# A fused attention and feed-forward kernel: plain float32 for fewer products, and a new order of work

## The chip, the cores and the metric

One core of a Trainium2 chip runs the whole program. It has five engines with a queue each: TensorE (PE, matmuls and transpositions into PSUM banks; its weight loads are listed as PEld), VectorE (DVE), ScalarE (ACT), GpSimd (POOL) and SyncE (SP, which here only issues transfers). An engine works through its queue in order, and an instruction that waits holds up everything behind it. The metric is the device time of one execution in microseconds (us), less being better.

## The reference

Block-causal attention over q, k, v of shape (8, 8, 576, 64), and on its output a feed-forward part with a convolution of three rows and a gate:

```python
scores = (1.0 / np.sqrt(D)) * np.matmul(q, k.transpose(0, 1, 3, 2))
mask = block_i >= block_j                       # blocks of 64 rows
scores = np.where(mask, scores, -1000000000.0)
attn = np.exp(scores - np.max(scores, axis=-1, keepdims=True))
attn = attn / (np.sum(attn, axis=-1, keepdims=True) + 1e-09)
x = np.matmul(attn, v)                          # heads side by side: (8, 576, 512)
h = np.maximum(x @ w_in, 0.0)                   # w_in (512, 1024)
conv_out = sum(conv_w[k] * hp[:, k:k + S, :] for k in range(3))
out = (h * (1.0 / (1.0 + np.exp(-conv_out)))) @ w_out   # w_out (1024, 512)
```

The three weight arrays come as 64-bit floating point numbers, q, k and v as float32.

## The kernel before

**Numbers in two halves.** TensorE reads a float32 operand either as plain float32 or under a rounded type, float32r. Where the kernel uses the rounded type it keeps an operand as a high half (rounded) and a low half (what rounding left), and adds three products: high by high, high by low, low by high. The tiles have names that end so: `wih`, `wil` are the halves of w_in, `woh`, `wol` of w_out, `ptah`, `ptal`, `ptbh`, `ptbl` of the transposed attention weights, `vv` holds the high half of v in columns 0 to 63 and the low half in 64 to 127.

**Visits.** The work goes pair by pair of heads, four pairs for each of the eight batch elements. The first batch element is done in two rounds, so that its feed-forward part can start early: in the first visits (part "A") each of the four pairs does its query rows 0 to 255, in the second visits (part "B") rows 256 to 575; the 28 pairs of the other batch elements have one visit each. A visit transposes q and k (`first_t`, `rest_t`, `stage_t`), forms the scores and exponentials (`stage_sa`, `stage_sb`, `stage_s`), normalizes them on POOL, transposes the weights back (`stage_x`, L1564) and multiplies them by v (`stage_pv`). Two first visits and two second visits work on both heads at once. In the first and second visits every product of q and k, and P V (L1648), is plain float32: `early` is true there. The later visits use halves (L1672, L1668).

**Feed-forward.** `ffn` runs for rows 0 to 254 of batch element 0 after its first visits, for its other rows after the second visits, then twice for each batch element. L1754 multiplies x by the halves of w_in (12 matmuls for each of eight chunks of 128 columns), ACT and DVE do the gate, POOL the low half `gl` (L1794), and L1820 multiplies by the halves of w_out.

**Weights.** `split` turns each 64-bit weight tile into halves. SP loads it (L1105, L1131), ACT takes absolute values (L976), POOL clamps (L982, for all but the first tile), DVE shifts bits (L987, L999, L1003, L1010), ACT writes the high half (L1045); then TensorE forms minus the high half (L1061) and the remainder (L1064) in a bank. For four of the sixteen tiles (`WPA`) it also adds the number itself by a plain float32 matmul (`all_`, L1070) and ACT writes the low half (L1073); for the others DVE adds the number while it writes the low half (L1067).

**The first loads.** The first 256 rows of q and k for all eight heads go into one tile under the name `ptbh`, and v into `ptbl` (`load_first`, L943, L954); TensorE transposes q and k as plain float32 against `ident` (L1260).

**What sets the order.** Every operation is entered in a plan (`pl.op`) with its engine, a duration, what it depends on, and the buffers it touches. `Plan.order` then places all of them: it keeps one list of ready operations for each engine and takes the one with the smallest due time from a table of numbers (`TARGETS`, one for each operation, in twentieths of a us). A PE operation whose mark `rows64` differs from that of the one before is lengthened by `switch` (0.2). Where the plan leaves PE idle for longer than `LEAST` (0.4 us), and a bank is free, it puts filling matmuls there, whose results nobody reads (`work`, L1969). So the order of each engine's queue is fixed before the program runs; what an instruction waits for on the chip is another matter.

Of the kernel before, what the change touches and what calls it, by code (L numbers as in the profile page):

```python
# [580 lines left out]
def kernel(  # L581
# [70 lines left out]
    QDV, KDV, RDV, ADV, BDV, LDV = (), (), (), (), (), False  # L652
    EA = True
    WPE = tuple(range(16))
    WPA = (0, 1, 2, 3)
    VAT = (0, 1, None, 0)
    FHP = ()
    ZDMA, APM, SHARE = True, True, {0: 2}
# [72 lines left out]
    def twin(tag):  # L731
# [4 lines left out]
        if len(hist) > cap:  # L736
            b.before = hist[-1 - cap]
# [1268 lines left out]
```

## Time and profile before

| | us |
|---|---|
| median of three runs | 757.05 |
| lowest and highest of them | 756.24, 759.91 |
| the profiled execution | 758.76 |
| its span, first to last instruction | 756.9 |
| TensorE busy | 748.3 |
| VectorE busy | 622.2 |
| ScalarE busy | 604.0 |
| GpSimd busy | 418.9 |
| ten filling matmuls of the start (L1969, `blank`) | 4.6 |
| twenty later ones (L1969, `rident`) | 6.6 |

The span begins with the first instruction, and the profiled execution's own time has 1.9 us around it. A row of the timeline gives the start in us, the length in us, the engine, the line, the operation, what it writes and reads, its shape, how many like it follow directly (x10), and in brackets the idle time before it with what ended that. Lengths of matmuls overlap, since they are pipelined; what one costs is read from the distance between starts. A plain float32 matmul shows as two records, one of the rounded type as one. A row of a group gives the count, then busy us and the mean ns of one, then idle us before.

### The profile page before, as it was taken

Reading aid. Unit: us, or ns where it says so; the run is one execution under the profiler, and the core shown is the slowest. Engines: PE = TensorE matmul, PEld = TensorE weight load, DVE = VectorE, ACT = ScalarE, POOL = GpSimd, SP = SyncE. Lnnn points to the kernel's source line nnn. Section 1 sums busy time; section 2 is a strip of 40 time slices with the busy share of each in tenths; the row PEclk is TensorE's granted clock in tenths of the full one; section 3 lists DMA queues with packets and bytes.
Section 4 is the critical chain, followed back from the end, with each engine's and each line's share of the span. In section 5 each row is a group of like instructions: output and inputs, shape, how many; then the busy total and the mean of one; then the engine's idle time right before and its main releaser. Section 6 shows DMA issues by size and latency. Waiting matters only on the chain.

```text
span 756.9 us, 16715 instructions
## 1 busy us (share of the span) xinstructions
PE 748.3 (99%) x5155; PEld 669.0 (88%) x5155; DVE 622.2 (82%) x1831; ACT 604.0 (80%) x1753; POOL 418.9 (55%) x630
## 2 busy tenths in 40 slices
PE   8899999999999999999999999999999999999998
PEld 5577789899999898999989899998989889898997
DVE  5879889998979788898979879898889879896541
ACT  6879979878979688797979679797978769786652
POOL 2435365666765546566565547556575655665321
PEclk9999999999999999999999999999999999999999
DMA  8754665577562555465454664555456544530001
GB/s 223 207 155 143 164 125 122 129 163 166 127 148 69 132 136 130 106 157 129 116 118 107 143 146 110 122 131 125 112 131 144 126 115 115 127 75 15 15 29 42
DMA packets 165628, 92.63 MB, mean 122 GB/s; under 512 B 134924, under 2 KB 142116, under 8 KB 165540
## 3 DMA queue, kind: packets, MB, share of 16 engines
q1 hardware_dynamic: 164996, 91.43, 49.6%
q8 instruction: 42, 0.69, 0.4%
q14 instruction: 46, 0.38, 0.2%
q10 hardware_dynamic: 544, 0.13, 0.1%
HBM read 38.30 MB, written 9.44 MB: 63 GB/s over the span
## 4 chain that ended last, share of the span: by engine, by line
PE 94%; ACT 2%; DVE 2%; POOL 1%; issue 0%; ACTq 0%; POOLq 0%
PE bank L1820 27%; PE bank L1754 26%; PE bank L1672 11%; PE bank L1564 8%; PE bank L1377 5%; PE bank L1375 4%; PE bank L1648 3%; PE bank L1329 3%; PE bank L1179 3%; PE bank L1969 1%; PE bank L1420 1%; PE bank L1061 1%; PE bank L1064 1%; DVE st L1496 0%; PE bank L1325 0%
## 5 line engine op out<-in xcount | busy, mean ns | idle before, releaser
L1754 PE MATMUL bank<-x,wih 128*128 128x290 f32 (+3 forms) x1024 | 200.9, 300 | 0.0
L1794 POOL TENSOR_TENSOR gl<-t,gh 128x289 fp32r<-128x289 f32 (+3 forms) x128 | 103.2, 811 | 127.6 <-ACT gh L1791 118.1
L1754 PEld LDWEIGHTS bank<-x,wih 128*128 128x128 f32 x1024 | 158.0, 189 | 3.5 <-issue 0.8
L1820 PE MATMUL bank<-woh,gh 128*128 128x512 f32 (+1 forms) x296 | 118.3, 400 | 0.0
L1820 PE MATMUL bank<-woh,gl 128*128 128x512 f32 (+1 forms) x296 | 115.0, 388 | 0.0
L1820 PE MATMUL bank<-wol,gh 128*128 128x512 f32 (+1 forms) x296 | 114.9, 388 | 0.0
L1754 PE MATMUL bank<-x,wil 128*128 128x290 f32 (+3 forms) x512 | 111.3, 299 | 0.0
L1385 DVE TENSOR_REDUCE st<-bank 128x1 f32<-128x128 f32 (+1 forms) x224 | 106.3, 482 | 2.9
L1578 DVE TENSOR_TENSOR ptbl<-bank,ptbh 128x512 fp32r<-128x512 f32 (+1 forms) x140 | 87.6, 631 | 5.5 <-ACT ptbh L1575 3.1
L1575 ACT ACTIVATE ptbh<-bank 128x512 fp32r<-128x512 f32 (+2 forms) x168 | 81.4, 503 | 9.5 <-PE bank L1564 8.7
L1775 DVE SCALAR_TENSOR_TENSOR t<-bank,cw,t 128x289 f32<-128x289 f32 (+3 forms) x128 | 64.8, 506 | 23.8 <-ACT t L1771 22.1
L1754 PEld LDWEIGHTS bank<-x,wil 128*128 128x128 f32 x512 | 82.3, 189 | 0.8 <-issue 0.4
L827 POOL TENSOR_SCALAR vv<-vn 128x320 fp32r<-128x320 f32 x56 | 25.7, 460 | 90.2 <-DMA vn<-in_v_dram 51.9
L1377 PE MATMUL bank<-kl,qz 128*128 128x128 f32 (+1 forms) x224 | 71.8, 322 | 0.0
L1820 PEld LDWEIGHTS bank<-woh,gl 128*128 128x128 f32 x296 | 55.5, 188 | 12.4
L1771 ACT ACTIVATE t<-bank,cw 128x289 f32<-128x289 f32 (+3 forms) x128 | 64.2, 501 | 2.7
L1779 DVE SCALAR_TENSOR_TENSOR t<-bank,cw,t 128x288 f32<-128x288 f32 (+3 forms) x128 | 64.1, 501 | 1.1
L1768 ACT ACTIVATE bank<-bank 128x290 f32<-128x290 f32 (+3 forms) x128 | 51.7, 404 | 15.6 <-PE bank L1754 14.6
L1791 ACT ACTIVATE gh<-t 128x289 fp32r<-128x289 f32 (+3 forms) x128 | 56.0, 444 | 8.9 <-DVE t L1787 7.9
L1784 ACT ACTIVATE t<-t 128x289 f32<-128x289 f32 (+3 forms) x128 | 56.9, 445 | 7.3 <-DVE t L1779 6.5
L1672 PE MATMUL bank<-ptbl,vv 128*64 128x192 f32 x224 | 61.5, 315 | 0.0
L1820 PEld LDWEIGHTS bank<-wol,gh 128*128 128x128 f32 x296 | 55.8, 189 | 5.6
(187 smaller groups left out, 2005.0 us busy)
## 6 DMA issues: line engine op xcount, KB each, us to landing
out_dram<-stage SPq DMA_DIRECT2D x35, 256.0 KB, 2.2
ka<-kh SPq DMA_DIRECT2D x56, 144.0 KB, 2.6
kb<-kh SPq DMA_DIRECT2D x56, 144.0 KB, 2.6
vn<-in_v_dram SPq DMA_DIRECT2D x58, 128.0 KB, 2.7
qnf<-in_q_dram SPq DMA_DIRECT2D x56, 128.0 KB, 2.4
knf<-in_k_dram SPq DMA_DIRECT2D x56, 128.0 KB, 2.7
x<-in_moe_w_out_dram SPq DMA_DIRECT2D x8, 512.0 KB, 4.4
qa<-qh SPq DMA_DIRECT2D x28, 144.0 KB, 2.4
```

Source lines behind the costliest of these rows:

```text
L1377: nc.tensor.matmul(sb.ap[:, 0:nk], qz.ap[:, z:z + 128], kl.ap[:, 0:nk], start=False, stop=True)
L1385: nc.vector.tensor_reduce(out=st.ap[:, i:i + 1], in_=sb.ap[:, 0:nk], op=ALU.max, axis=AX.X, negate=True)
L1564: nc.tensor.matmul(tb.ap[0:kk, col:col + P].bitcast(F32R), pb[x].raw[:, 128 * c:128 * c + kk], rident, start=(z == 0), stop=True, is_trans ...
L1575: nc.scalar.activation(out=hi(), in_=src(), func=AF.Copy)
L1578: nc.vector.tensor_tensor(out=lo(), in0=src(), in1=hi(), op=ALU.subtract)
L1672: nc.tensor.matmul(tb.ap[0:m, q0 - qa:qb - qa], vv.ap[:, chunk(c), w[ps_]], pm.ap[:, 128 * c + q0:128 * c + qb] if qa == 0 else pm.ap[:, c ...
L1754: nc.tensor.matmul(fb.ap[:, 0:n2], wt[:, c, fs], xs[c][xi].ap[:, x0:x0 + n2], start=(n + c - c0 == 0), stop=(n + c - c0 == 3 * NCC - 1))
L1771: nc.scalar.activation(out=t.ap[:, 0:no], in_=fb.ap[:, own:own + no], func=AF.Copy, scale=cw[:, NFC + f:NFC + f + 1])
L1775: nc.vector.scalar_tensor_tensor(out=t.ap[:, i0:no], in0=fb.ap[:, own + i0 - 1:own + no - 1], scalar=cw[:, f:f + 1], in1=t.ap[:, i0:no], o ...
L1779: nc.vector.scalar_tensor_tensor(out=t.ap[:, 0:i1], in0=fb.ap[:, own + 1:own + 1 + i1], scalar=cw[:, 2 * NFC + f:2 * NFC + f + 1], in1=t.a ...
L1794: nc.gpsimd.tensor_tensor(out=gbuf[1].ap[:, f, carry:carry + no], in0=t.ap[:, 0:no], in1=gbuf[0].ap[:, f, carry:carry + no], op=ALU.subtract)
L1820: nc.tensor.matmul(fb.ap[:, 0:cut], gbuf[a].ap[:, f, cs], w[:, f, ds], start=(f == 0 and n == 0), stop=(f == NFC - 1 and n == 2))
```

## The change

The table `TARGETS` is new throughout, so that the order differs on every engine from the start to shortly before the end. Beside it:

- `PRB`: in the second visits only pairs 0 and 1 keep the plain float32 P V. Pairs 2 and 3 get halves of the weights and of v: v is loaded into `vn`, POOL writes its halves into `vv` in three cuts of rows, ACT writes the high half of the transposed weights, and the low half comes either from DVE or (for the two blocks of 384 and 512 columns, `EBLK`) from a matmul that subtracts the high half in the bank (`sub`) and an ACT copy. P V is then three passes.
- `WPA` is empty: no plain float32 matmul for weight tiles (`all_`) is left, and DVE writes all low halves (`fl2`).
- The first q and k lie where the exponentials of the second visits go later (from `p2` on), under two names, float32 and float32r; they are transposed under the second. The first exponentials of `p2`, `p3`, `p4` wait for those transpositions.
- `rows64` gets a value for each kind of plain float32 matmul (2 or 3), so that the plan counts `switch` at every change of type; before it did so only around the scores of the first two rounds. The plan's time for a transfer of a w_in tile goes from some 1.6 to 1.9 us.
- New branches with `SRAW` or `PRA` false aren't taken.

Instructions over the whole program, before and after: plain float32 matmuls of P V 56 and 36, of weight sums 5 and 0; rounded matmuls for P V of the second visits 0 and 56, subtractions (`sub`) 0 and 8; filling matmuls 30 and 36; transpositions of the first q and k 16 and 16 (plain, then rounded); low-half copies of attention weights on ACT 0 and 8, of w_in tiles on ACT 5 and 0, their additions on DVE 4 and 9; passes over v on POOL 112 and 124; transfers on SP 769 and 769.

```diff
-139 133 161 153 228 245 108 134 154 173 261 282 282 276 548 557 342 446 499 534 561 522 556 540 613 602 185 233 212 248 362 494 247 263 252 264 271 254 321
...
-    WPA = (0, 1, 2, 3)
+    WPA = ()
     VAT = (0, 1, None, 0)
+    SRAW, PRA, PRB = True, True, (0, 1)
...
+    qkt = [nc.alloc_sbuf_tensor_at(f"qk{x}", [P, 2, 2, H, D], d, offset=at0).ap() for x, d in (("f", F32), ("r", F32R))]
+    firstq = Bin([])
...
+        elif tag in ("p2", "p3", "p4"):
+            b.before = firstq
...
-        vn = vraw(VAT[p]) if part else one([P, 5, 2, D], F32, "vn")
+        vn = vraw(VAT[p]) if part and p in PRB else one([P, 5, 2, D], F32, "vn")
...
+        if part and p not in PRB:
+            return halves((0, 1), VCUT)
...
-        bufs, vbufs = [[late(j, hh) for hh in range(2)] for j in range(2)]
+        bufs, vbufs = [firstq], [late(1, hh) for hh in range(2)]
...
-        ld = pl.op(SP, 0.4 if f < NFC else 1.0, go, (at - WLEAD if f >= NFC else WL0 + WLS * f) + JD[f], deps=deps, bufs=bufs, xfer=c_dma(P * 4096 // share, 1024) if f < NFC else 2.1)
+        ld = pl.op(SP, 0.4 if f < NFC else 1.0, go, (at - WLEAD if f >= NFC else WL0 + WLS * f) + JD[f], deps=deps, bufs=bufs, xfer=1.9 / share if f < NFC else 2.1)
...
-                    nc.tensor.transpose(tb.ap[:, c * P:(c + 1) * P],
-                                        x()[:, c, 2 * p:2 * p + 2, :].rearrange("p j d -> p (j d)"), ident)
-
-            o = pl.op(PE, 0.22, tr, at, deps=lds[p], bufs=buf + [tb], area=0.49)
+                    nc.tensor.matmul(tb.ap[:, c * P:(c + 1) * P].bitcast(F32R),
+                                     x()[:, c, 2 * p:2 * p + 2, :].rearrange("p j d -> p (j d)"), rident, start=(c == 0), stop=True,
+                                     is_transpose=True, skip_group_check=True)
+
+            o = pl.op(PE, run(*[tr_()] * 2), tr, at, deps=lds[p], bufs=buf + [tb], area=0.7)
...
-                      area=0.85, rows64=True)
+                      bufs=sb + [t[x] for x in (("q", "k") if SRAW else ("qa", "qb", "kh", "kl"))], area=0.85, rows64=3 if SRAW else 1)
...
+        raw = PRA if part == "A" else p in PRB if early else False
...
-            if early:
+            if raw:
...
+            def sub():
+                nc.tensor.matmul(src(), nident, hi(), start=False, stop=True, skip_group_check=True)
+
+            def ev_lo2():
+                nc.scalar.activation(out=lo(), in_=src(), func=AF.Copy)
+
             e1 = pl.op(ACT, c_act(n) + 0.02, ev_hi, t0 + 0.3, deps=[o], bufs=[tb] + bufs_hi)
-            e2 = pl.op(DVE, c_dve(n, two_in=True), ev_lo, t0 + 0.5, deps=[e1], bufs=[tb] + bufs_hi + bufs_lo)
+            if sub_ok:
+                e2 = pl.op(PE, run(mm_(n)), sub, t0 + 0.4, deps=[e1], bufs=[tb] + bufs_hi)
+                e2 = pl.op(ACT, c_act(n), ev_lo2, t0 + 0.5, deps=[e2], bufs=[tb] + bufs_lo)
+            else:
+                e2 = pl.op(DVE, c_dve(n, two_in=True), ev_lo, t0 + 0.5, deps=[e1], bufs=[tb] + bufs_hi + bufs_lo)
...
-        passes = (("a", P, 0), ("h", 64, 1))
+        raw = part and not isinstance(vvd[0], Buf)
+        passes = (("h", 64, 0), ("l", 64, 0), ("h", 64, 1)) if early else (("a", P, 0), ("h", 64, 1))
...
-            if early:
+            if raw:
                 v_, vbufs, vdone = vvd
...
                     o = pl.op(PE, run(*[y for c in half for y in mf_(qb - max(128 * c, qa), 64)]), mm, at + (0.3 if qa else 0),
-                              deps=[o] + vdone + [e for x_ in need for e in x_], bufs=vbufs + [tb, pts[0]], area=0.44)
+                              deps=[o] + vdone + [e for x_ in need for e in x_], bufs=vbufs + [tb, pts[0]], area=0.44, rows64=2)
```

What the new table does to the order is shown at three places. The first is the head of TensorE's queue, from the start to the scores of the first pair. A row has the line, the operation, what it writes and reads, and the shape; L1969 and L1260 are the fillings and the first transpositions, L1478 the scores. Before:

```order
L1969 MATMUL bank<-blank 128x512 x10
L1260 MATMUL bank<-ident,ptbh 128x128 x4
L1969 MATMUL bank<-rident 128x512 x2
L1478 MATMUL bank<-kh,qa 128x128 x2
L1482 MATMUL bank<-maskt,rident 64x64 x2
L1478 MATMUL bank<-kh,qa 128x256 x2
L1482 MATMUL bank<-maskt,rident 64x64 x2
```

In the change L2085 are the fillings, L1326 the first transpositions, L1098 and L1101 two steps of a weight tile (L1061 and L1064 before), L1578 the scores:

```order
L2085 MATMUL bank<-blank 128x512 x14
L1326 MATMUL bank<-rident,qkr 128x128 x2
L2085 MATMUL bank<-rident 128x512 x7
L1098 MATMUL bank<-wih,nident 128x512
L1101 MATMUL bank<-wil,rident 128x512
L2085 MATMUL bank<-rident 128x512 x3
L1098 MATMUL bank<-wih,nident 128x256
L1326 MATMUL bank<-rident,qkr 128x128 x4
L1578 MATMUL bank<-kh,qa 128x128 x2
L1582 MATMUL bank<-maskt,rident 64x64 x2
L1578 MATMUL bank<-kh,qa 128x256 x2
```

Ahead of the first scores stand 24 filling matmuls in place of 12, and one and a half weight tiles in place of none. The second place is the head of SP's queue, which goes with it: loads of q and k (L943, in the change L952) and of w_in (L1105, in the change L1142). Before:

```order
L943 DMA ptbh<-in_q_dram 128x2x64 x2
L1105 DMA gh<-in_moe_w_in_dram 128x2x256
L943 DMA ptbh<-in_q_dram 128x2x64
L943 DMA ptbh<-in_k_dram 128x2x64
L943 DMA ptbh<-in_q_dram 128x2x64
L943 DMA ptbh<-in_k_dram 128x2x64
L1105 DMA gh<-in_moe_w_in_dram 128x4x256
L1105 DMA gl<-in_moe_w_in_dram 128x4x256
```

and in the change:

```order
L1142 DMA gh<-in_moe_w_in_dram 128x4x256
L952 DMA qkf<-in_q_dram 128x2x64 x2
L1142 DMA gh<-in_moe_w_in_dram 128x2x256
L1142 DMA gl<-in_moe_w_in_dram 128x4x256
L952 DMA qkf<-in_k_dram 128x2x64 x2
L952 DMA qkf<-in_q_dram 128x2x64 x2
L952 DMA qkf<-in_q_dram 128x4x64 x2
```

A load of 512 KB (128x4x256) has moved ahead of the first load of q, and the loads of w_in otherwise come earlier among those of q and k. The third place is POOL around the normalizations of the fourth pair's first visit (p0f and p1f with st_139, L1519; in the change st_141, L1619), and the clamps of weight tiles (L982, in the change L1019). Before:

```order
L982 TENSOR_SCALAR stage<-stage 128x512
L982 TENSOR_SCALAR gh<-gh 128x512
L982 TENSOR_SCALAR gl<-gl 128x512
L982 TENSOR_SCALAR gh<-gh 128x512
L1519 TENSOR_SCALAR p0f_91<-p0f_91,st_139 128x128
L1519 TENSOR_SCALAR p1f_95<-p1f_95,st_139 128x256
L1519 TENSOR_SCALAR p0f_93<-p0f_93,st_139 128x128
L1519 TENSOR_SCALAR p1f_97<-p1f_97,st_139 128x256
L1456 TENSOR_SCALAR p3f_103<-p3f_103,st_133 128x512
```

and in the change:

```order
L1019 TENSOR_SCALAR gh<-gh 128x512
L1019 TENSOR_SCALAR gl<-gl 128x512
L1619 TENSOR_SCALAR p0f_91<-p0f_91,st_141 128x128
L1619 TENSOR_SCALAR p1f_97<-p1f_97,st_141 128x256
L1619 TENSOR_SCALAR p0f_93<-p0f_93,st_141 128x128
L1619 TENSOR_SCALAR p1f_95<-p1f_95,st_141 128x256
L1019 TENSOR_SCALAR gh<-gh 128x512
L1019 TENSOR_SCALAR stage<-stage 128x512
```

Before, the clamps of a w_out tile and three w_in tiles stood right ahead of those four normalizations, the last of them (`gh`) that of the sixth such tile that POOL clamps; in the change two w_in tiles do, and the sixth stands behind them.

More of the change, by code (lines that the diff above doesn't have):

```diff
@@ L725 @@
         twins[tag] = []
+        at0 = at if tag == "p2" else at0
         for i in range(cap):
@@ L1247, in stage_t, with first_h, tr, ev_hi @@
         return t, ready, ready4
+    def first_h(nq, nk, p, at):
+        t = {nm: two([P, S], F32R, nm) for nm in (("kh", "kl") if p < 2 else ("ka", "kb")) + ("qa", "qb")}
+        if p >= 2:
+            t["kh"], t["kl"] = t.pop("ka"), t.pop("kb")
+        firstk.append((t["kh"], t["kl"]))
+        es = []
+        for (x, buf, lds), hi, lo, scale in ((nq, t["qa"], t["qb"], SCALE), (nk, t["kh"], t["kl"], 1.0)):
+            tb = bank("tv")
+            def tr(x=x, tb=tb):
+                for c in range(2):
+                    nc.tensor.matmul(tb.ap[:, c * P:(c + 1) * P].bitcast(F32R),
+                                     x()[:, c, 2 * p:2 * p + 2, :].rearrange("p j d -> p (j d)"), rident, start=(c == 0), stop=True,
+                                     is_transpose=True, skip_group_check=True)
+            def ev_hi(tb=tb, hi=hi, scale=scale):
+                nc.scalar.activation(out=hi.ap[:, 0:Q1], in_=tb.ap[:, 0:Q1], func=AF.Copy, scale=scale)
+            def ev_lo(tb=tb, hi=hi, lo=lo, scale=scale):
+                nc.vector.scalar_tensor_tensor(out=lo.ap[:, 0:Q1], in0=tb.ap[:, 0:Q1], scalar=scale,
+                                               in1=hi.ap[:, 0:Q1], op0=ALU.mult, op1=ALU.subtract)
+            o = pl.op(PE, run(*[tr_()] * 2), tr, at, deps=lds[p], bufs=buf + [tb], area=0.7)
+            o = pl.op(ACT, c_act(Q1), ev_hi, at + 0.3, deps=[o], bufs=[tb, hi])
+            es += [o, pl.op(DVE, c_dve(Q1, two_in=True), ev_lo, at + 0.6, deps=[o], bufs=[tb, hi, lo])]
+        return t, (es, es), []
     def first_t(nq, nk, p, at):
+        if not SRAW:
+            return first_h(nq, nk, p, at)
         t = {"q": two([P, S], F32, "qa"), "k": two([P, S], F32, "kh" if p < 2 else "ka")}
@@ L1264, in first_t, with rest_h, mv4 @@
+            o = pl.op(PE, run(*[tr_()] * 2), tr, at, deps=lds[p], bufs=buf + [tb], area=0.7)
             es.append(copy_op(dve, Q1, lambda hi=hi: hi.ap[:, 0:Q1], lambda tb=tb: tb.ap[:, 0:Q1], at + 0.3, [o], [tb, hi], scale))
         return t, (es, es), []
+    def rest_h(nat, at):
+        t = {nm: two([P, S], F32R, nm) for nm in ("qa", "qb")}
+        t["kh"], t["kl"] = firstk.pop(0)
+        (t["qz"], z1), (t["qdl"], z2) = keep([P, 2 * S], F32R, "qz", 2, 0.0, at - QZ), keep([P, P], F32R, "qdl", 2, 0.0, at - QZ)
+        es, ready4 = [], []
+        (nq, lq), (nk, lk) = nat
+        parts = ((((0, nq, 2), (P, nq, 3), (2 * P, 64, 4)), [lq, lk], [nq], ((0, 0, Q1, 320), (1, 320, 512, 64))),
+                 (((0, nk, 2), (P, nk, 3)), [lk], [nk], ((1, 0, Q1, 256),)))
+        both = naturals(parts, nq, (t["qa"], t["qb"], t["kh"], t["kl"]), (at, at + 0.5))
+        for which in range(2):
+            hi, lo = (t["qa"], t["qb"]) if which == 0 else (t["kh"], t["kl"])
+            t0 = at + 0.5 * which
+            es += both[which]
+            if which == 0:
+                for src, dst, c_ in ((hi, t["qz"], S - 64), (lo, t["qdl"], 0)):
+                    for o_ in (0, 64):
+                        def mv4(o_=o_, src=src, dst=dst, c_=c_):
+                            nc.sync.dma_start(out=dst.ap[o_:o_ + 64, c_ + o_:c_ + o_ + 64].bitcast(F32),
+                                              in_=src.ap[o_:o_ + 64, S - 64:S].bitcast(F32))
+                        ready4.append(pl.op(SP, 0.65, mv4, t0 + 2.0, deps=es[0:1] + z1 if src is hi else es[1:2] + z2, bufs=[src, dst],
+                                            xfer=0.1))
+        return t, es, ready4 + es
@@ L1417, in mm @@
                 qs = slice(128 * i, 128 * i + 128)
-                for hh in range(2):
-                    r = slice(64 * hh, 64 * hh + 64)
-                    nc.tensor.matmul(sb[hh].ap[:, 0:nk], t["q"].ap[r, qs], t["k"].ap[r, 0:nk], start=True, stop=True)
+                prods = (("q", "k"),) if SRAW else (("qa", "kh"), ("qb", "kh"), ("qa", "kl"))
+                for n, (q_, k_) in enumerate(prods):
+                    for hh in range(2):
+                        r = slice(64 * hh, 64 * hh + 64)
+                        nc.tensor.matmul(sb[hh].ap[:, 0:nk], t[q_].ap[r, qs], t[k_].ap[r, 0:nk], start=(n == 0),
+                                         stop=(n == len(prods) - 1))
                 for hh in range(2):
@@ L1475, in go @@
                 for i in tiles:
[L1476 to L1479 removed]
+                    prods = (("q", "k"),) if SRAW else (("qa", "kh"), ("qb", "kh"), ("qa", "kl"))
+                    for n, (q_, k_) in enumerate(prods):
+                        for hh in range(2):
+                            r = slice(64 * hh, 64 * hh + 64)
+                            nc.tensor.matmul(sb[hh].ap[:, 128 * i:384 * i + 128 - 128 * i], t[q_].ap[r, 128 * i:128 * i + 128],
+                                             t[k_].ap[r, 0:128 * (i + 1)], start=(n == 0), stop=(n == len(prods) - 1))
                     for hh in range(2 * APM):
@@ L1592, in flat @@
         def flat(j):
-            return lambda: ta[j].ap
+            return lambda: ta[j].ap.rearrange("p (c n) -> p c n", n=P) if part == "A" and EA and not raw else ta[j].ap
         def fourth(pb, done):
-            pp = ptr if early else ptb[0]
+            pp = ptr if raw else ptb[0]
             e5 = one_bank([(4, 4, 64, 0)], 64, P, lambda: pp.ap[0:64, :, 3, 0:64], lambda: pp.ap[64:P, :, 3, 0:64],
@@ L1628, in stage_pv @@
         early = part is not None
-        vv, vdone = (None, None) if early else vvd
+        vv, vdone = (None, None) if part and not isinstance(vvd[0], Buf) else vvd
         o64 = 64 * hh
         done = []
-        passes = (("a", P, 0), ("h", 64, 1))
+        raw = part and not isinstance(vvd[0], Buf)
+        passes = (("h", 64, 0), ("l", 64, 0), ("h", 64, 1)) if early else (("a", P, 0), ("h", 64, 1))
         w = {"h": slice(0, D), "l": slice(D, P), "a": slice(0, P)}
@@ L1891, in values @@
         else:
-            vvd[i] = first_v(first[2], p // 2)[2 * (p % 2):2 * (p % 2) + 2]
+            if PRA:
+                vvd[i] = first_v(first[2], p // 2)[2 * (p % 2):2 * (p % 2) + 2]
+            else:
+                vvd[i] = split_v(first[2], p // 2, at) if p % 2 == 0 else vvd[i - 1]
     values(0, -20.0)
@@ L1940 @@
                     fetch(i + 2, b0 + ot + NLEAD)
-            x = stage_x(sm, hh, b0 + ox + jx, part, x[4] if x else None)
+            x = stage_x(sm, hh, b0 + ox + jx, part, x[4] if x else None, p)
             flush()
```

75 lines of the change are left out of this document (49 added, 26 removed), and 434 rows, old and new, of the table TARGETS.

## The prediction

> **What bounds the kernel now.** I read the page's busy table first, then the busy time by stretches of the span, then TensorE's timeline.
>
> ```profile
> span 756.9 us, 16715 instructions
> PE 748.3 (99%) x5155; PEld 669.0 (88%) x5155; DVE 622.2 (82%) x1831; ACT 604.0 (80%) x1753; POOL 418.9 (55%) x630
> ...
> 0.00:20.00 20.00, 17.34 (x94) 11.53 (x94) 10.27 (x36) 13.61 (x40) 5.49 (x17) 1.00 0.78 213
> 20.00:40.00 20.00, 17.62 (x101) 11.38 (x101) 16.63 (x49) 16.99 (x53) 9.38 (x15) 1.00 0.83 223
> ...
> 60.00:80.00 20.00, 20.00 (x140) 14.78 (x137) 18.77 (x46) 18.54 (x53) 9.85 (x15) 1.00 0.38 106
> ...
> 200.00:300.00 100.00, 100.00 (x694) 91.11 (x692) 84.33 (x253) 80.93 (x236) 60.08 (x88) 1.00 0.53 127
> ```
>
> In each row of stretches the columns are length, then busy us (count) of PE, PEld, DVE, ACT and POOL. From 200 us on TensorE (PE) is busy for 100.00 of 100 us, and its starts follow each other at the matmul's own pace (below: a 512-column matmul every 0.23 us). There, only fewer or cheaper matmuls, or fewer losses between them, shorten the program. In the first 40 us PE is busy for 35 us, but part of that is filling matmuls (L1969), whose results nobody reads. The waits of PE in the first 45 us, in us, times and longest:
>
> ```profile
> PE bank L1564 <- POOL p0f L1519: 1.7, 1, 1.7
> PE bank L1564 <- POOL p1f L1519: 1.1, 2, 0.6
> PE bank L1969 <- DVE blank L821: 1.1, 1, 1.1
> PE bank L1064 <- DVE wil L1010: 0.4, 1, 0.4
> PE bank L1969 <- ACT kh L832: 0.3, 1, 0.3
> ```
>
> The first two rows of the next fence are PE around the longest of these, the third is the first matmul of the feed-forward part (FFN), and the last three are ACT and POOL at that place.
>
> ```profile
> 33.72 2.00 PE L1969 MATMUL bank<-rident 128*128 128x512 f32 x7
> 37.38 0.28 PE L1564 MATMUL bank<-rident,p0r 128*128 128x128 f32 x1 [1.66 <-POOL p0f L1519]
> ...
> 41.42 0.63 PE L1754 MATMUL bank<-x,wih 128*128 128x256 f32 x2
> ...
> 35.16 0.66 ACT L976 ACTIVATE gh<-gh 128x512 f32<-128x512 f32 x1 [1.56 <-DMA gh<-in_moe_w_in_dram]
> ...
> 35.91 0.61 POOL L982 TENSOR_SCALAR gh<-gh 128x512 f32<-128x512 f32 x1 [1.61 <-DVE st L1332]
> 36.50 0.82 POOL L1519 TENSOR_SCALAR p0f<-p0f,st 128x128 f32<-128x128 f32 x1
> ```
>
> ACT stood 1.56 us at the head of its queue for a weight load; POOL's clamp of that same tile (35.91, behind ACT's 35.16) stood ahead of the normalization `p0f`; PE waited for that one. Seven fillings and two waits (1.7 and, right after, 0.6) make over 4 us without useful work, and then comes a slow stretch (its last columns are granted clock, DMA share, GB/s):
>
> ```profile
> 40.10:43.50 3.40, 3.40 (x13) 2.35 (x11) 2.75 (x9) 2.60 (x10) 2.81 (x4) 0.50 0.86 216
> ```
>
> At clock 0.50 these 3.4 us did the work of 1.7.
>
> **The change part by part.** *Weight sums.* Five plain float32 matmuls (three of 512 columns, two of 256) leave PE, and ACT's copies of their results become additions on DVE.
>
> ```profile
> 26.73 1.02 PE L1070 MATMUL bank<-gl,ident 128*128 128x512 f32 x2
> 27.19 0.62 PE L1564 MATMUL bank<-rident,p0r 128*128 128x128 f32 x1
> 27.65 0.32 PE L1564 MATMUL bank<-rident,p1r 128*128 128x128 f32 x2
> ```
>
> One such matmul is two records. It and one transposition take 26.73 to 27.65, 0.92 us; a transposition is at most 0.13 (three from 80.36 to 80.75, below), so 0.79 to 0.9, and I take 0.85. Three and two halves: 3 x 0.85 + 2 x 0.43 = 3.4 us. All five stand ahead of 41.42.
>
> *P V of pairs 2 and 3 in the second visits.* Four heads go from plain float32 to split operands.
>
> ```profile
> 79.14 1.29 PE L1648 MATMUL bank<-ptbh,vn 128*64 128x320 f32 x4
> 80.36 0.46 PE L1179 MATMUL bank<-rident,knr 128*128 128x128 f32 x3
> 80.75 1.19 PE L1648 MATMUL bank<-ptbh,vn 128*64 128x320 f32 x6
> 81.87 1.13 PE L1420 MATMUL bank<-ka,qa 64*128 64x512 f32 x4
> ...
> 68.34 2.27 PE L1648 MATMUL bank<-ptbh,vv 128*64 128x320 f32 x10
> 70.54 0.51 PE L1754 MATMUL bank<-x,wih 128*128 128x256 f32 x2
> ...
> 300.59 0.33 PE L1672 MATMUL bank<-ptbl,vv 128*64 128x320 f32 x1
> 300.75 0.19 PE L1668 MATMUL bank<-ptbh,vv 128*128 128x64 f32 x1
> 300.78 0.34 PE L1672 MATMUL bank<-ptbl,vv 128*64 128x320 f32 x1
> 300.96 0.39 PE L1820 MATMUL bank<-woh,gh 128*128 128x512 f32 x1
> 301.19 0.40 PE L1820 MATMUL bank<-wol,gh 128*128 128x512 f32 x1
> ```
>
> Out: 80.36 - 79.14 plus 81.87 - 80.75, 2.34 us a head, 9.4 for four. In, per head: nine matmuls of 320 columns at 0.16 to 0.18 (300.59, 300.78), three of 192 at 0.10 and two of 64 at 0.03, 1.9 us, and two subtractions of 512 and 384 columns at 0.23 and 0.17: 2.3 us, 9.2 for four. Net -0.2 us; by columns alone (0.45 ns each) it would be -1, with every head's first weight load bare about +0.5. I take -0.2.
>
> *Fewer changes of type.* The same five float32 matmuls take 2.34 us as two groups and 70.54 - 68.34 = 2.20 as one, so a group of its own costs PE at least 0.14 us. Counting runs of float32 rows in the order: 24 before the first FFN matmul and 20 after it, in the change 16 and 12. That is 8 x 0.14 = 1.1 us on each side of it; 0.19 each would give 1.5.
>
> *Transpositions of the first q and k* under the rounded name: 16, of which four end within 0.70 us (5.79 below), so they cost at most 2.8 now. They lie in front of waits; I take 0.
>
> *ACT, DVE, POOL.* ACT gains eight low-half copies and loses five weight copies, DVE gains five additions and four low halves, POOL twelve passes over v.
>
> ```profile
> L905 POOL TENSOR_TENSOR vv<-vn,vv 128x320 fp32r<-128x320 f32 x56 | 49.2, 879 | 3.6
> L827 POOL TENSOR_SCALAR vv<-vn 128x320 fp32r<-128x320 f32 x56 | 25.7, 460 | 90.2 <-DMA vn<-in_v_dram 51.9 <-PE bank L1672 28.0 <-PE bank L1329 3.4
> L832 ACT ACTIVATE ptbh<-bank 128x512 f32<-128x512 f32 x12 | 7.0, 595 | 0.1
> L1073 ACT ACTIVATE wil<-bank 128x512 fp32r<-128x512 f32 x3 | 1.8, 595 | 0.0
> L1067 DVE TENSOR_TENSOR wil<-bank,gl 128x512 fp32r<-128x512 f32 x2 | 1.4, 686 | 0.6 <-PE bank L1064 0.6
> ```
>
> POOL: two pairs of two heads at 0.88 + 0.46 a head, 5.4 us; ACT eight copies of at most 0.60 less five, of which three are 0.60, some +2 us; DVE nine of at most 0.69, up to +6 us. They hide behind PE, which works through both kinds of second visit without a wait from 45 us on; the cover is thin on ACT and DVE (18.5 and 18.8 of 20 us at 60 to 80).
>
> *The start.* SP now issues a 512 KB weight load ahead of q, with 14 fillings ahead of the first transposition, and the place of seven fillings has one.
>
> ```profile
> 1.05 4.63 PE L1969 MATMUL bank<-blank 128*128 128x512 f32 x10 [1.05 <-DVE blank L821]
> 5.79 0.70 PE L1260 MATMUL bank<-ident,ptbh 128*128 128x128 f32 x4
> 7.63 0.46 PE L1478 MATMUL bank<-kh,qa 64*128 64x128 f32 x3
> ```
>
> Of the 41.4 us up to the FFN, 1.05 is the lead-in, 4.6 the ten slow fillings, 4.6 twenty at 0.23 (300.96 to 301.19), 3.5 the waits of the list that are left (1.7, 1.1, 0.4, 0.3); 27.7 remain for everything else. Less 3.4 and 1.1 that is 23.2. The change adds 1.05, fourteen slow fillings (6.5) and 22 at 0.23 (5.1): 35.8 with no such wait, 39.3 with the same 3.5. The two waits at 37.38 (2.3 us) go, since pair 3's normalizations now stand ahead of the sixth weight tile's clamp on POOL: about 37.0, so **-4.4 us**. What is late next are the exponentials of pair 3 on ACT. Ends: 33 if the small waits inside the 23.2 (an estimate: some 3 us) go too, 46.8 for the third rival.
>
> *The half-clock stretch* after 41.42 loses (43.5 - 41.4) / 2 = 1.0 us. It follows on the waits above; I take half, -0.5, between 0 and -1.7. The Trainium skill (TensorE: Matmul & The Clock Gate, What's actually happening) has the clock fall after an idle window of about 3.4 us, and windows that run free of the kernel. Here it fell after a stretch whose longest wait was 1.66 us, so the trace differs; by the page nothing would be lost or won there.
>
> Sum: -4.4 - 0.5 - 1.1 - 0.2 = -6.2 us. The profiled execution took 758.76 us (span 756.9 and 1.9 around it), so 752.6 for it; it lies 1.7 above the median of 757.05, and from that the forecast is **750.8 us**, with its own range 747 to 753.
>
> **The rivals.**
> (1) *ACT and DVE bind in the second visits.* For it: 94% and 93% busy at 60 to 80 us, 2 us more for ACT, and an earlier FFN that asks for its activations sooner. Against: behind the one filling in row 78 the new order has none, and the program puts one wherever its plan leaves PE idle for over 0.4 us. It would give back some 4 of the 4.4 us: 754.8.
> (2) *The start is not bound by PE at all* and the change doesn't do what it says there: six more fillings fill what the sums left, and FFN starts at 41 again. For it: PE's 5 idle us in the first 40 and 36 planned fillings. Then only what comes after counts, -1.3: 755.8. The Trainium skill (Perfetto Trace Analysis, Identifying the Most-Contended Engine) holds matmul busy time a bad measure and weight-load busy time a better one; PEld's 11.5 of 20 us here against 18.2 of 20 later agrees, and speaks for this rival.
> (3) *Slower: q behind the weights.* The 512 KB load goes first on SP's queue, and the fillings ahead of the first scores rise from 12 to 24. If the first scores come at 13 instead of 7.63 and the four pairs then need the same 33.8 us (7.63 to 41.42), as a chain of exponentials, normalizations and transpositions, FFN starts at 46.8: +5.4, less 1.3 behind it: 761.1. It decides if the first scores come after about 8.9 (7.63 + 1.3) and the four pairs are not faster. Against: the sums that stood between them are gone.
> (4) *Better:* the small waits go too and no half-clock stretch is left: 33 instead of 41.4, -8.4 - 1.0 - 1.5 = 746.
>
> **How the numbers follow.** Forecast 0.56, rival (1) 0.16, (2) 0.11, (3) 0.06, (4) 0.11. The order of the steady part is new as well; with PE at its own pace there I give it 2 us either way. About 0.5% (3.8 us) is what a measurement of this kernel can tell from no change: faster is below 753.3, slower above 760.8. Faster: the forecast, (4) and a third of (1) and (2), less its tail: 0.74; slower, most of (3): 0.05; within 0.5%: 0.21. The range that holds 8 in 10 leaves out half of (4) and (3): 744.8 to 756.2.
>
> **What would show it.** The first FFN matmul at 35 to 39 us and no wait of PE on a normalization over 1 us (else rival 2 or 3); the first scores before 12 us; no stretch at clock 0.50 after 10 us; PE without waits over 0.5 us from 45 to 120 us (else rival 1); groups of split P V near 2 us a head; the stretch 200 to 300 us as full as now. FFN at 41 us or later, or PE waiting for ACT's low halves at 60 to 110 us, makes the prediction wrong.

## The result, and the profile after

| | before | after |
|---|---|---|
| median, four runs each (us) | 757.27 | 766.78 |
| lowest and highest | 756.24, 759.91 | 765.97, 768.84 |
| ratio, 95% interval | | 1.0125 [1.0097, 1.0152] |
| profiled execution, and its span | 758.76, 756.9 | 767.02, 765.2 |
| first scores start at | 7.63 | 18.54 |
| first FFN matmul starts at | 41.42 | 47.17 |

The change made the kernel 9.5 us slower; the forecast was 6.2 us faster. TensorE's work did not grow. Here are the page's busy line of the changed kernel and its busy time by stretches (length, then busy us and count of PE, PEld, DVE, ACT, POOL, then granted clock, DMA share, GB/s):

```profile
PE 748.2 (98%) x5175; PEld 672.3 (88%) x5175; DVE 628.4 (82%) x1840; ACT 605.2 (79%) x1754; POOL 426.7 (56%) x642
...
0.00:20.00 20.00, 12.45 (x46) 9.12 (x47) 6.36 (x22) 5.70 (x12) 2.20 (x8) 0.90 0.72 200
20.00:40.00 20.00, 18.80 (x120) 12.62 (x120) 17.85 (x54) 17.55 (x61) 8.28 (x17) 0.93 0.54 152
...
200.00:300.00 100.00, 98.89 (x699) 90.97 (x699) 84.17 (x250) 80.63 (x236) 58.76 (x87) 1.00 0.51 122
```

Busy PE is 748.2 us against 748.3, so the longer span is time in which PE stands still: in the first 20 us PE is busy for 12.45 us where it was 17.34, DVE for 6.36 where it was 10.27, and ACT for 5.70 where it was 13.61. The stretch from 200 to 300 us, full before, lacks 1.1 us. What PE waited for in the first 60 us of the changed kernel, and SP's queue beside it (us, times, longest):

```profile
PE bank L1326 <- DMA qkf<-in_k_dram: 6.0, 2, 3.3
PE bank L2085 <- DVE blank L829: 1.0, 1, 1.0
...
SPq L952 <- PE bank L1326: 4.4, 1, 4.4
```

SP stands 4.4 us ahead of a load of q or k because of a transposition, and PE stands 6.0 us ahead of transpositions because of loads. The timeline of PE shows where:

```profile
9.42 0.47 PE L1326 MATMUL bank<-rident,qkr 128*128 128x128 f32 x2 [2.77 <-DMA qkf<-in_k_dram]
9.68 3.12 PE L2085 MATMUL bank<-rident 128*128 128x512 f32 x7
...
17.72 0.51 PE L1326 MATMUL bank<-rident,qkr 128*128 128x128 f32 x4 [3.28 <-DMA qkf<-in_k_dram]
18.54 0.49 PE L1578 MATMUL bank<-kh,qa 64*128 64x128 f32 x4 [0.31 <-ACT kh L840]
...
47.17 0.47 PE L1867 MATMUL bank<-x,wih 128*128 128x256 f32 x2
```

The two transpositions at 9.42 are those of the first pair's q; the transfer they waited for is a load of k, and not one whose data they read. Seven fillings behind the wait take 3.12 us, where the seven at 33.72 took 2.00 before. The granted clock there is 0.50; these are the two slow stretches:

```profile
9.00:12.40 3.40, 2.98 (x9) 2.43 (x10) 1.52 (x4) 1.96 (x5) 0.59 (x1) 0.50 0.27 62
...
19.20:22.70 3.50, 3.50 (x15) 2.53 (x11) 2.42 (x8) 2.36 (x12) 0.00 (x0) 0.51 0.58 138
```

Each stands around or behind one of the two waits. The program's own list of waits tells why a q transposition waits for k. The number behind the engine is the row's place in its queue, where equal rows that follow each other count as one; DMAHW0 to DMAHW7 are the eight semaphores of landed transfers, PE and DVE those of the engines:

```
changed kernel
PE 3  L1326 MATMUL bank<-rident,qkr 128x128 [waits DMAHW2_49,DMAHW3_49,DMAHW1_49,DMAHW4_49,DMAHW0_49,DMAHW7_49,DVE_49,PE_49]
SP 8  L952 DMA qkf<-in_q_dram 128x2x64 [waits DMAHW2_49,PE_49]
twelve pairs of names (a run below)
PE 3  L1328 MATMUL bank<-rident,qkr_114 128x128 [waits DMAHW4_49,DVE_49,PE_49]
SP 9  L954 DMA qkf_115<-in_q_dram 128x2x64 [waits DMAHW2_49]
```

The changed kernel writes under one name (`qkf`) and reads under another (`qkr`) that covers the same 8 KB of each partition. The first transposition waits for six transfer semaphores. They stand for all seven loads put there ahead of it (two of them count on the same semaphore), whatever part each fills. And the next load of q waits for the transposition, though it fills another part. In the kernel before, which writes and reads under one name, each transposition waits for its own load alone. This was theory **T1: the two names are followed as a whole**, so that loads and transpositions alternate.

Its rivals were **T2** (the 512 KB weight load ahead of q, the forecast's rival 3), **T3** (the rounded transposition itself is slow) and **T4** (the new table's order later on costs waits of its own, which would explain the 1.1 us above).

### The profile page after: what moved, and what is told of

Read it like the earlier page. It is cut to its first block, busy times and chain, and to the rows that moved or that the text cites. A ratio compares the mean times of both kernels' runs of the same rounds, so it can differ in the third digit from the quotient of the medians.

```text
span 765.2 us, 16814 instructions
## 1 busy us (share of the span) xinstructions
PE 748.2 (98%) x5175; PEld 672.3 (88%) x5175; DVE 628.4 (82%) x1840; ACT 605.2 (79%) x1754; POOL 426.7 (56%) x642
## 4 chain that ended last, share of the span: by engine, by line
PE 77%; ACT 11%; DVE 5%; DMA 3%; issue 2%; POOL 1%; SPq 0%; ACTq 0%; DVEq 0%; POOLq 0%
PE bank L1933 25%; PE bank L1867 21%; PE bank L1785 10%; PE bank L1665 6%; PE bank L1470 4%; PE bank L1472 4%; PE bank L1423 3%; PE bank L1216 2%; DMA qkf<-in_k_dram 2%; DMA x<-in_moe_w_out_dram 2%; ACT ptbh L1676 1%; DVE st L1480 1%; ACT p4f L1439 1%; DVE t L1888 1%; ACT t L1884 1%
## 5 line engine op out<-in xcount | busy, mean ns | idle before, releaser
L1480 DVE TENSOR_REDUCE st<-bank 128x1 f32<-128x128 f32 (+3 forms) x224 | 106.5, 481 | 2.8
L1676 ACT ACTIVATE ptbh<-bank 128x384 fp32r<-128x384 f32 (+2 forms) x180 | 87.1, 503 | 11.6 <-PE bank L1665 10.7
L835 POOL TENSOR_SCALAR vv<-vn 128x320 fp32r<-128x320 f32 (+2 forms) x62 | 28.5, 461 | 82.1 <-DMA vn<-in_v_dram 29.3
L1472 PE MATMUL bank<-kl,qz 128*128 128x128 f32 (+2 forms) x224 | 71.7, 322 | 0.0
L1785 PE MATMUL bank<-ptbl,vv 128*64 128x192 f32 x240 | 64.5, 314 | 0.0
L1900 DVE SCALAR_TENSOR_TENSOR t<-t,bank 128x289 f32<-128x289 f32 (+3 forms) x128 | 57.0, 446 | 6.0 <-ACT t L1897 4.9
```

Source lines behind the costliest of these rows:

```text
L1472: nc.tensor.matmul(sb.ap[:, 0:nk], qz.ap[:, z:z + 128], kl.ap[:, 0:nk], start=False, stop=True)
L1480: nc.vector.tensor_reduce(out=st.ap[:, i:i + 1], in_=sb.ap[:, 0:nk], op=ALU.max, axis=AX.X, negate=True)
L1676: nc.scalar.activation(out=hi(), in_=src(), func=AF.Copy)
L1785: nc.tensor.matmul(tb.ap[0:m, q0 - qa:qb - qa], vv.ap[:, chunk(c), w[ps_]], pm.ap[:, 128 * c + q0:128 * c + qb] if qa == 0 else pm.ap[:, c ...
L1900: nc.vector.scalar_tensor_tensor(out=t.ap[:, 0:no], in0=t.ap[:, 0:no], scalar=1.0, in1=fb.ap[:, own:own + no], op0=ALU.add, op1=ALU.mult)
```

## The experiments

Ratios are to the kernel before, timed beside each run; its median moved between 757.27 and 758.33 us. Each run of this section but the one named "k first" either keeps the order of all five queues of the kernel that it starts from, or changes only due times of operations from 150 us on.

**One name, plain float32** (on the changed kernel):

```diff
-            res.append((lambda z=z: qkt[1][:, z], bufs, lds[z]))
+            res.append((lambda z=z: qkt[0][:, z], bufs, lds[z]))
...
-                    nc.tensor.matmul(tb.ap[:, c * P:(c + 1) * P].bitcast(F32R),
-                                     x()[:, c, 2 * p:2 * p + 2, :].rearrange("p j d -> p (j d)"), rident, start=(c == 0), stop=True,
-                                     is_transpose=True, skip_group_check=True)
+                    nc.tensor.transpose(tb.ap[:, c * P:(c + 1) * P],
+                                        x()[:, c, 2 * p:2 * p + 2, :].rearrange("p j d -> p (j d)"), ident)
```

> The changed kernel with one edit: the 16 first transpositions read q and k under the name under which they were loaded, as plain float32; the order of all five queues stays. T1 (TensorE's first transposition and SP's next loads wait for each other because the two names of one memory are followed as a whole): the first scores come at 11 to 12.5 us in place of 18.54, the first FFN matmul at 38 to 40 in place of 47.17, the time falls by some 8 us to 757 to 760. T2 (the 512 KB weight load ahead of q is what makes them late): first scores at 16 or later, time 764 or more. T4 (the waits on exponentials and halves after 45 us belong to the new order): of what T1 leaves, the 2.8 us of waits after 200 us stay.

Measured: 758.41 us, ratio to before 1.0010 [0.9992, 1.0028]; first scores at 11.37, first FFN matmul at 39.13, as T1 had it. Of the waits after 200 us, 2.1 us stay.

**Twelve pairs of names** (on the changed kernel), one for each load, transposed as rounded:

```diff
-    qkt = [nc.alloc_sbuf_tensor_at(f"qk{x}", [P, 2, 2, H, D], d, offset=at0).ap() for x, d in (("f", F32), ("r", F32R))]
+    qkt = {(z, c, g): [nc.alloc_sbuf_tensor_at(f"qk{x}{z}{c}{g}", [P, 2 * n, D], d, offset=at0 + 4 * D * (H * (2 * z + c) + 2 * p0)).ap()
+                       for x, d in (("f", F32), ("r", F32R))]
+           for z in range(2) for c in range(2) for g, (p0, n) in enumerate(((0, 1), (1, 1), (2, 2)))}
```

> The changed kernel with one edit: twelve pairs of names, one for each load of the first q and k, in place of one pair for all; transpositions stay rounded and the order of all queues stays. T1: as the run with plain reading, within 1 us of it: first scores at 11 to 12.5 us, first FFN matmul 38 to 40, time 757 to 760. T2: first scores at 16 or later, 764 or more. If the rounded type itself were slow (T3), this run stays at 766 while the one with plain reading gains.

Measured: 758.57 us, 1.0012 [1.0002, 1.0022]. PE's timeline in this run:

```profile
1.05 5.30 PE L2087 MATMUL bank<-blank 128*128 128x512 f32 x14 [1.05 <-DVE blank L831]
6.41 0.37 PE L1328 MATMUL bank<-rident,qkr 128*128 128x128 f32 x2
...
10.28 0.45 PE L1328 MATMUL bank<-rident,qkr 128*128 128x128 f32 x4
11.04 0.49 PE L1580 MATMUL bank<-kh,qa 64*128 64x128 f32 x4 [0.31 <-ACT kh L842]
...
38.65 0.47 PE L1869 MATMUL bank<-x,wih 128*128 128x256 f32 x2
```

No transposition waits for a transfer any more, and the first scores come at 11.04 in place of 18.54, with the same order and the same weight load ahead of q. T1 holds, T2 falls: 1.0125 against 1.0012 is 1.1%, 8.6 us. The plain run and this one are equal, so T3 falls too.

**One pair of names in the kernel before**: the changed kernel's lines for `qkt` and `firstq` and its rounded transposition, nothing else.

```diff
-        qk = Buf(cp, [P, 2, 2, H, D], F32, "ptbh")
+    qkt = [nc.alloc_sbuf_tensor_at(f"qk{x}", [P, 2, 2, H, D], d, offset=at0).ap() for x, d in (("f", F32), ("r", F32R))]
...
-            res.append((lambda z=z: qk.ap[:, z], bufs, lds[z]))
+            res.append((lambda z=z: qkt[1][:, z], bufs, lds[z]))
```

> The kernel before with one edit: its first q and k go under one pair of names, float32 and float32r, and are transposed as rounded; the order of all queues stays that of before. T1: slower, since the first transposition now waits for seven loads and two pairs of later loads wait for transpositions: first scores at 9.5 to 13 us in place of 7.63, time 759 to 765. T2: no pair of names matters, 757.3 within 1.

Measured: 765.89 us, 1.0107 [1.0091, 1.0124], and first scores at 13.39, both a little over their ranges. What PE waited for in its first 45 us:

```profile
PE bank L1266 <- DMA qkf<-in_q_dram: 5.5, 1, 5.5
PE bank L1266 <- DMA qkf<-in_k_dram: 2.3, 1, 2.3
```

The first FFN matmul starts at 48.12. One small part of the change, put into the kernel before, makes nearly the whole loss.

**Twelve pairs in the kernel before**: the same with a pair for each load, by the `qkt` lines of the run with twelve pairs.

> The kernel before with the rounded transpositions, but with twelve pairs of names, one for each load. T1: the false waits are gone, so first scores at 7.3 to 8 us and 757 within 1. T3 (the rounded type itself costs): slower by as much as the run with one pair of names.

Measured: 757.34 us, 0.9993 [0.9977, 1.0009]; first scores at 7.38, first FFN matmul at 39.72. T1 as expected: without false waits the new name costs nothing.

T1 explains 8.6 us, which would leave the changed kernel level with before, not 6 us ahead. The next runs ask where the rest is. The longest waits of PE after 150 us, in the run with twelve pairs of names:

```profile
PE bank L1667 <- DVE ptal L1681: 0.8, 1, 0.8
PE bank L1425 <- ACT p1f L1485: 0.7, 1, 0.7
PE bank L1425 <- ACT p2f L1485: 0.7, 1, 0.7
PE bank L1667 <- ACT p3f L1485: 0.4, 1, 0.4
PE bank L1472 <- DVE t L1902: 0.3, 1, 0.3
```

The kernel before has one there, of 0.2 us.

**The old later order** on the run with twelve pairs: 5033 of the 6425 due times, those of the operations that the old plan starts at 150 us or later, are the old table's values for the same operations plus 80 twentieths. One line of the table:

```diff
-9706 9705 9718 9731 9664 9762 9780 9797 9824 9800 9894 9904 9757 9762 9780 9788 9791 9796 9816 9829 9840 9858 9884 9895 9916 9950 9804 9816 9818 9829 9843 9845 9858 9863 9879 9906 9937 9948 9962 10008
+9719 9728 9731 9736 9746 9766 9778 9799 9812 9821 9901 9911 9751 9768 9773 9779 9787 9797 9805 9819 9830 9857 9872 9889 9921 9964 9801 9806 9833 9853 9862 9868 9878 9893 9909 9923 9943 9958 9987 10036
```

> The run with own names, and the due times of all operations from 150 us on taken from the table of before, each 4 us later (the plan's own shift between the two): the order of the later part is that of before again. T4 (the new table's order from there on costs waits): the waits on ACT and DVE at 320, 487, 631 and 679 us go and the lead of some 5 us over the kernel before that stands at 145 us is kept to the end: 3 to 5 us under the run with own names, 753.5 to 755.5. T5 (an earlier start is eaten by ACT and DVE whatever the order): 758.6 within 1, the lead shrinks as before.

Measured: 754.90 us, 0.9972 [0.9962, 0.9982]: faster than both kernels, within the expected range. Busy time from 480 to 700 us in the kernel before, with twelve pairs and the new order, and with the old later order:

```profile
480.00:700.00 220.00, 219.87 (x1562) 203.27 (x1562) 185.96 (x553) 177.67 (x521) 130.95 (x197) 1.00 0.46 111
```

```profile
480.00:700.00 220.00, 217.87 (x1544) 200.87 (x1543) 184.86 (x546) 176.10 (x511) 128.18 (x192) 1.00 0.47 111
```

```profile
480.00:700.00 220.00, 219.97 (x1569) 203.81 (x1568) 184.19 (x546) 176.29 (x514) 130.65 (x195) 1.00 0.46 112
```

The 2.1 us that PE lacks in the second are back in the third, with 25 more matmuls in the same time.

**The new later order in the kernel before**, the same edit the other way (the new table's values less 80).

> The kernel before with one edit: the due times of all operations from 150 us on come from the new table, each 4 us earlier; start, first and second visits stay as before. T4: the waits of the new order come with it, 3 to 5 us slower than before: 761 to 763. T5: 757.8 within 1.

Measured: 761.15 us, 1.0039 [1.0025, 1.0053]. T4 holds in both directions: 0.39% (3.0 us) from the kernel before to this one, and 0.40% between 1.0012 and 0.9972.

**The old later order on the changed kernel**, one pair of names and all.

> The changed kernel as it is, with its one pair of names and so its false waits, but with the old order from 150 us on. If the two causes add (T1 and T4): 766.8 less 3.6, 762.5 to 764, the first FFN matmul at 46.5 to 47.5 as in the changed kernel, and no wait of TensorE over 0.6 us after 200 us. If the later waits only come of the late start: 766.8 within 1.

Measured: 764.77 us, 1.0088 [1.0072, 1.0104], first FFN matmul at 47.78, and no wait of PE left after 200 us. The time is 0.8 us over the expected range and the FFN 0.3; the kernel before took 758.33 beside it, and by the ratio the edit is worth 0.37% (2.8 us). So the two causes add.

The table shows the same by place. It gives how much later than in the profiled execution of before the n-th of the 1536 matmuls of x by w_in starts (in us, from the starts of those records in each trace; before, they start at 41.42, 192.46, 399.79, 532.53 and 738.13):

| | 1st | 261st | 693rd | 981st | last |
|---|---|---|---|---|---|
| changed kernel | +5.75 | +5.09 | +5.61 | +6.58 | +8.38 |
| twelve pairs of names | -2.77 | -4.52 | -3.10 | -2.05 | -0.11 |
| the same, old later order | -2.71 | -4.18 | -3.66 | -3.68 | -3.76 |
| one pair, old later order | +6.37 | +4.43 | +5.39 | +5.34 | +5.22 |
| before, profiled again | -3.07 | -1.90 | -1.88 | -1.93 | -2.06 |
| before, one pair | +6.71 | +5.91 | +5.95 | +5.96 | +5.88 |
| before, twelve pairs | -1.70 | -2.20 | -2.36 | -2.29 | -2.32 |
| before, new later order | -2.45 | +0.81 | +1.13 | +2.08 | +3.36 |

With the old later order what stands at the 261st stands at the end within some 0.8 us, mostly within 0.3; with the new one 2.5 to 4.4 us are lost on the way. In the last row another 3.3 us are lost ahead of the 261st: some 2 of them are a wait of PE at 53.21, in a part whose order is that of before. The row "before, profiled again" shows that the first profile of before is a late one by 2 us.

**The kernel before, profiled twice more**, unchanged.

> The kernel before, unchanged, profiled once more. If the wait of 1.66 us on the normalization at 37.38 and the stretch at clock 0.50 behind it belong to the kernel, they are there again and the first FFN matmul starts at 41.4 within 0.3. If they belonged to one execution, at least one of the two is gone and the FFN starts at 39 to 40.5, as in the run of before with twelve pairs of names.

> As the run ahead of it, a third profile of the kernel before: the same two outcomes.

Measured: 756.69 and 757.28 us. The FFN starts at 38.35 and 38.47, a little sooner than both outcomes had it. In these two profiles the wait of 1.66 us at 37.38 and the half clock behind it are gone. The first of the two has the same seven fillings with no wait behind them, and at 40.10 a granted clock of 1.00:

```profile
33.90 2.00 PE L1969 MATMUL bank<-rident 128*128 128x512 f32 x7
35.74 0.22 PE L1564 MATMUL bank<-rident,p0r 128*128 128x128 f32 x1
...
40.10:43.50 3.40, 3.39 (x23) 2.45 (x21) 3.24 (x8) 2.92 (x6) 3.40 (x5) 1.00 0.52 117
```

In the same profile, PE's first FFN matmul and its next long wait, and what ACT did ahead of that:

```profile
38.35 0.40 PE L1754 MATMUL bank<-x,wih 128*128 128x256 f32 x2
```

```profile
52.24 0.50 PE L1061 MATMUL bank<-woh,nident 128*128 128x512 f32 x1 [1.58 <-ACT ka L832]
```

```profile
51.09 0.66 ACT L976 ACTIVATE stage<-x 128x512 f32<-128x512 f32 x1 [2.34 <-DMA x<-in_moe_w_out_dram]
```

So in these executions the start is 3 us sooner, and 1.6 us (in the other 2.2) are lost again at 52, behind a load of w_out that lands late. The waits at 37.38 and the 41.42 stand in one profile of three.

The half clock did not belong to one execution. The mean granted clock of each execution is on record, and one stretch of 3.4 us at 0.50 takes 0.002 from it (1.7 of 757 us). Of the 51 executions of the kernel before that were timed beside these runs, 34 have a mean of 0.998 or less, as the first profile has; their median is 758.19 us. The other 17 have 0.999 or 1.000, as the two further profiles have, and a median of 757.19. The stretch can stand elsewhere, too: in the kernel before with the new later order, whose start is that of before, the clock is 0.51 from 53.40 to 56.80, behind a wait of PE of 2.13 us at the same w_out step. Without the false waits the new start has it seldom: with the plain name, with twelve pairs, and with twelve pairs and the old later order, 26 of 27 executions have 0.999 or 1.000.

**k first** (on the run with twelve pairs and the old later order): due times of the first pair's chain moved ahead, and a limit on one group of fillings. The first line of the table, and the limit:

```diff
-219 209 325 302 354 325 246 281 286 295 371 375 506 444 710 738 354 406 519 734 553 576 526 591 650 559 328 325 411 393 578 563 408 432 411 482 459 473 436 462
+219 209 325 302 354 325 180 185 286 295 371 375 506 444 710 738 354 406 519 734 553 576 526 591 650 559 328 325 329 330 578 563 340 372 351 422 399 413 376 402
...
+        k = min(k, 5) if len(fills) == 1 else k
         fills.append(k)
```

> The run with own names and the old later order, with one more edit at the start: the first pair's k is transposed ahead of its q and both ahead of the first weight tile, and 5 fillings stand there in place of 16, so that the first scores come at 8 to 9 us in place of 11.13. T6 (the start is a chain of ACT and DVE work that begins with the first scores, both over 90% busy from 12 to 40 us): the first FFN matmul comes 1.5 to 3 us sooner than 38.71 and the time falls to 752.5 to 753.5. T7 (FFN waits for weights and for the sum of the work, not for the first scores): FFN at 38 to 39.5, 754.9 within 0.7.

Measured: 761.84 us, 1.0044 [1.0028, 1.0059]: neither theory's number. PE's timeline:

```profile
1.05 3.78 PE L2031 MATMUL bank<-blank 128*128 128x512 f32 x8 [1.05 <-DVE blank L774]
4.89 0.37 PE L1271 MATMUL bank<-rident,qkr 128*128 128x128 f32 x1
5.45 0.37 PE L1271 MATMUL bank<-rident,qkr 128*128 128x128 f32 x1 [0.19 <-DMA qkf<-in_k_dram]
5.62 2.46 PE L2031 MATMUL bank<-rident 128*128 128x512 f32 x5
...
9.29 0.76 PE L1523 MATMUL bank<-kh,qa 64*128 64x128 f32 x3
...
43.17 0.40 PE L1812 MATMUL bank<-x,wih 128*128 128x256 f32 x2
```

The first scores came at 9.29, 1.8 us sooner than in the run that it started from and later than meant, and the FFN came 4.5 us later. The new due times moved more than the first pair's chain: 18 records of second-visit scores and their masks (L1462, L1466) now stand ahead of the FFN where there were 12, and 8 matmuls with minus the high half of a weight tile (L1043) where there were 6. So the run doesn't say whether the first scores bind the start. That stays open.

## Why the prediction was wrong

**The step that failed** is the one on the transpositions of the first q and k: "they cost at most 2.8 now. They lie in front of waits; I take 0." It priced the instructions under their new name and not the waits that the name brings. Those cost 8.6 us of time (1.0125 to 1.0012), through 6.0 us of waits and two stretches at clock 0.50. The list of waits of the built program held it already: a q transposition with six transfer semaphores.

**The start** had the first FFN matmul at 37.0, and 35 to 39 as what would show it right: it came at 47.17. Without the false waits it comes at 38.65. That this lies inside the band is chance, for nothing is gained: the kernel before has it at 38.35 and 38.47 in its two further profiles. The term of -4.4 took the waits at 37.38 (2.3 us) for the kernel's, and neither further profile has them. The fillings ahead of them do belong to the kernel (33.90 above). The term for the half clock, -0.5 with the stretch counted in half of the executions, holds up better: by the mean clocks two thirds of the executions of before have such a stretch, worth 1.0 us between the medians, and one of 27 has it once the false waits are gone. The step from the profiled execution to the median, 1.7 us less for both kernels, could not mend the start: the changed kernel has no wait at 37.38 to lose.

**The weight sums** were priced at 3.4 us. In the further profile the ten records and what lies between their starts and the next ones make 2.5 us: the mechanism was right, the size a third too large (the quoted pair stood beside a change of type, which was counted elsewhere). By the same reckoning the run with twelve pairs spends, ahead of the FFN, 1.1 us on a head of P V that stood behind it before, 1.1 on six more fillings (the forecast had 2.4) and 0.9 more in waits of PE, and 0.9 less on the first transpositions. What the eight fewer changes of type gave there is not told apart.

**P V and types** were to give 1.3 us behind the FFN. From the further profile of before to the run with the old later order the time behind the first FFN matmul shrinks by 2.1 us (754.8 - 38.35 = 716.5 against 753.1 - 38.71 = 714.4), of which 1.1 is that head: 1.0 is left, near the forecast. By the second further profile, with 0.5 us more of waits there, it is 1.4. (Waits of PE behind the FFN sum to about 2.0 us in the first one and in the run.) One split head is shown here, from the run with twelve pairs:

```profile
78.38 0.71 PE L1787 MATMUL bank<-ptbh,vv 128*64 128x320 f32 x4
...
79.54 0.42 PE L1787 MATMUL bank<-ptbl,vv 128*64 128x192 f32 x2
79.80 0.33 PE L1690 MATMUL bank<-ptbh,nident 128*128 128x384 f32 x1
79.97 0.46 PE L1787 MATMUL bank<-ptbl,vv 128*64 128x320 f32 x2
80.27 0.40 PE L1869 MATMUL bank<-x,wih 128*128 128x256 f32 x2
```

78.38 to 79.80 and 79.97 to 80.27 are 1.7 us; with two subtractions (0.17 here, and 0.23 by the forecast's price) that is 2.1, near the 2 us a head that was to show it right, against 2.34 for a plain one.

**The steady part** was given 2 us either way, and "as full as now" as the sign. It lost 3.0 us, by five waits of PE of 0.3 to 0.8 us, four of them on exponentials and halves. The order was new, and nothing in the forecast looked into it past 120 us.

**The rivals.** Rival 1 (ACT and DVE bind in the second visits) is small: from 45 to 150 us the changed kernel has two waits of PE over the 0.5 us that were its sign (0.7 and 0.6, both on ACT), and the run with twelve pairs one, of 0.6. Rival 2 (the start does not gain, only what comes after counts) has the outcome right once the false waits are gone, by the 38.4 of the further profiles rather than by 41.42; it gave 755.8, and the run with the old later order took 754.90. Rival 3 had the sign, the condition (first scores after 8.9) and nearly the place of the FFN (46.8 forecast, 47.17 measured), but not the cause: with twelve pairs of names the 512 KB weight load still goes first, no transposition among the first shown waits for a transfer, and first scores at 11.04, well after 8.9, still give an FFN at 38.65. The rival's "same 33.8 us" for the four pairs was 28.6 in the changed kernel and 27.6 there. Rival 4 needed the gain at the start and more, and falls with it.

In all, 8.6 us for the false waits, 3.0 for the later order and -2.1 for all other parts together (0.9972, -0.28%) make the +9.5 that was measured. They must, being steps of one chain of runs from the changed kernel to the one with both causes taken out. What bears them out is that the same edits elsewhere gave the same: the names 1.14% in the kernel before (1.0107 against 0.9993), the later order 0.39% there and 0.37% on the changed kernel.

## What to carry to other kernels

When one memory gets a second name, read the waits of the first instructions under it: here both names were followed as a whole, and one pair of names for each transfer took the 8.6 us back without any other edit. Before a wait in a trace is counted as a gain, see whether it returns in a second profile of the same program, and what the mean clocks of the other executions say: here 3 us of the start did not return, while the slow stretch was common. A new order of a stage that TensorE already fills has little to win, so keep that stage's old order when only the start is to change: that gave the fastest version here, 754.90 us, 0.28% under the kernel before.

## What the runs showed of the hardware

**TensorE starts slow, for longer or shorter, and the column of granted clock doesn't show it.** In the kernel before, and with twelve pairs of names, the fillings of 512 columns start 0.43 us apart up to 5.05, and in the latter 0.23 apart from 5.29 on. In the run with k first, with a wait of 0.19 us at 5.45, they are still 0.43 apart at 7.45, and the next row starts at 7.88. Here is that stretch, with a granted clock of 1.00:

```profile
5.00:8.00 3.00, 2.81 (x9) 2.03 (x9) 0.43 (x2) 0.95 (x2) 0.61 (x1) 1.00 1.04 304
```

Whether that short wait prolonged it wasn't tried.

The Trainium skill (TensorE: Matmul & The Clock Gate, What's actually happening) has the array at half its clock until a window of about 3.4 us was busy, by windows that run free of the kernel. The distances of the first two, slow from 1.05 to some 5.2, agree with it; the third, slow from 1.05 to 7.88, needed more than one such window.

**The granted clock fell to 0.50 behind waits shorter than 3.4 us, but not behind all of them.** The Trainium skill (the same section) has the clock fall after a window of about 3.4 us without work. The traces differ: in the changed kernel the clock fell behind a wait of 2.77 us, and the slow stretch lasted 3.40 us (9.00 to 12.40 above). In the kernel before with the new later order a wait of 2.13 us was followed by such a stretch, while in the second further profile the wait of 2.25 us at the same step was not (granted clock 1.00 from 53 to 60).

**The plain transposition is no dearer.** Sixteen first transpositions as plain float32 or as rounded gave 1.0010 and 1.0012.
